# Attention and MoE on one core: first-block outputs with queries on partitions, held and rationed MoE work

## The chip, the cores and the metric

The kernel runs on one core of a Trainium2 chip. The metric is the device time of that core in microseconds (us), the median of several executions. Engines are TensorE (PE; PEld is its weight load), VectorE (DVE), ScalarE (ACT), GpSimd (POOL) and SyncE (SP, which only issues DMAs here). A DMA is a transfer between DRAM and the memory on the core; it is issued by an engine and lands some us later. Results of matmuls stand in PSUM, a part of that memory. On one core an execution is called slow when it lies over 1.5% above the fastest of its kernel; such runs are left out of every ratio.

## The reference, cut to what matters

```python
# q, k, v: [8 batches, 8 heads, 576, 64]; f: [8, 8, 576]; w_in: [512, 2048]; w_out: [2048, 512]
scores = q @ k.T / sqrt(64) + (cum[i] - cum[j])      # cum = cumsum(log(clip(f)))
scores = where(j > i, -1e9, scores)
attn   = exp(scores - max) / (sum + 1e-9)
x      = (attn @ v) as [8 * 576, 512]
out    = silu(x @ w_in) @ w_out                      # float32, [4608, 512]
```

The decay is folded into per-key weights `w`: v is multiplied by `w`, and the softmax denominator is the sum of `w * exp(score)`.

## The kernel before: the parts that matter

The 576 queries of a batch are split: the first 128 (the "first block") of all eight batches are done early, two or four batches at a time, so that the MoE (here the two matmuls with w_in and w_out and the silu between them) has input early; the other 448 are done in a main loop of 16 quads (a quad is four heads of one batch, two quads to a batch). In between the scores of a quad, the function `fill(us)` emits MoE work: first-matmul chunks ("hp": four matmuls, then tanh on ACT, then the product "gt" on VectorE) and second-matmul parts ("po": four matmuls of 512 columns). Each engine's instructions stand in its queue in the order in which this program emits them. Scores and attention outputs share two PSUM tiles; hp, po and a few others share four PSUM buffers.

```python
    def out0(b):                     # first block: features on partitions
        dn = psc.tile([P, 2, 512], FP32, name="dn0", tag="sc")
        ...                          # 24 matmuls: 8 denominators broadcast to 32 rows, 16 halves of v
        nc.vector.reciprocal(out=rec, in_=dn[:, 0 : 2 * P])          # 128 x 256
        nc.vector.tensor_tensor(out=xg(g)..., in0=dn[:, 2 * P : 6 * P]..., in1=rec..., op=ALU.mult)

    def step():                      # one chunk of MoE work
        a, c = at["m1"], at["m2"]
        can1 = a < len(M1) and M1[a][0] in ready        # first matmul: group's x was emitted
        ...
        if can1 and can2:
            f1 = M1[a][1] / NFC                         # share done of the first-matmul group
            f2 = (c - sum(M2_OF[:g2])) / M2_OF[g2]      # share done of the second-matmul group
            can1 = f1 <= f2 or g1 > g2 + 1
        ...

    FILL = 2.6
    for m in range(NQ):              # main loop, one quad each
        n = 2 * m
        scores(n, 0); scores(n, 1); prepare(n);     fill(FILL)       # (joined lines)
        scores(n, 2); scores(n + 1, 0); prepare(n + 1); fill(FILL)
        scores(n + 1, 1); scores(n + 1, 2);         fill(FILL + 1.0)
        finish_quad(m)               # attention matmuls, denominator to SBUF, two reciprocals of 128 x 224
        fill(FILL)
        for e in range(2):
            divide(m, e, nc.gpsimd)  # x = numerator * reciprocal, on POOL
        if m % 2 == 1:
            ready.add(REST_OF[m // 2])                  # from here on, hp of this batch may be emitted
            ...
```

The loads, in the order in which POOL issues them: q and k of the first four blocks, the first half of w_in, (v of the first blocks is scaled), q and k of blocks 4 and 5, the other half of w_in, all of w_out. After w_out has landed, SP starts loading for the main loop.

The softmax here doesn't subtract the row's maximum and nothing guards it: scores larger than these inputs give would overflow.

## Time and profile before

| | before |
|---|---|
| time, median | 405.99 us (4 runs) |
| span of the profiled run (an execution of 404.22 us, not one of the four) | 402.4 us |
| TensorE busy | 349.2 us, 87% |
| first MoE matmul | 27.63 us |
| first scores of the main loop | 80.3 us |
| from there to the end | 322.1 us |

The page's first part gives busy time, share of the span and number of instructions of each engine. Its second part cuts the span into 40 slices; a digit is a share in tenths, and PEclk is the TensorE clock that was granted.

```profile
PE 349.2 (87%) x3682; PEld 192.7 (48%) x3717; DVE 208.6 (52%) x310; ACT 235.7 (59%) x408; POOL 151.7 (38%) x252
...
PEclk9958999999969999996999899999899989999999
```

TensorE has the most work, but an eighth of its span is idle, and the clock is below full in many slices all along the kernel. The list of waits of TensorE says what ended its idle time (engine, line, what it waited for: us in total, times, longest).

```profile
PE hp L478 <- POOL x L460: 20.5, 14, 2.7
...
PE hp L478 <- DVE x L321: 4.9, 2, 4.0
```

The first line is the largest: 20.5 us before first-matmul chunks, waiting for x, the product on POOL; the second, 4.9 us, is the same for the first blocks, where VectorE makes x. The timeline around one such wait (start us, duration us, engine, line, operation, count, and in brackets the idle time before with what ended it):

```profile
107.03 0.61 PE L429 MATMUL dn<-u,vp 128*32 128x128 bf16 x24
...
107.65 2.97 DVE L452 RECIPROCAL rec<-rec 128x224 f32<-128x224 f32 x2 [4.16 <-ACT rec L444]
108.10 0.40 PE L398 MATMUL sc<-qkT 64*128 64x128 bf16 x8 [0.46 <-ACT nm L447]
...
108.84 0.50 PE L478 MATMUL hp<-x,w_in_bf 128*128 128x384 bf16 x2
...
110.79 2.73 POOL L460 TENSOR_TENSOR x<-nm,rec 128x384 bf16<-128x384 f32 x4 [3.66 <-DVE rec L452]
112.06 0.48 PE L478 MATMUL hp<-x,w_in_bf 128*128 128x384 bf16 x1 [2.72 <-POOL x L460]
...
113.29 4.32 PE L478 MATMUL hp<-x,w_in_bf 128*128 128x384 bf16 x13 [0.75 <-POOL x L460]
```

The attention matmuls end at 107.6. Nothing but two sets of scores stands before the first chunk that needs the result. The two reciprocals take 2.97 us, POOL begins at 110.79, and TensorE stands still for 2.72 and 0.75 us. Then the thirteen matmuls from 113.29 take 4.32 us, 0.33 us each; in an undisturbed stretch sixteen of the same shape take 2.77 us, 0.17 each. A table of stretches (length; busy us of PE, PEld, DVE, ACT, POOL; clock; DMA share; GB/s) shows why:

```profile
105.00:110.00 5.00, 3.85 (x99) 2.35 (x98) 2.35 (x2) 3.94 (x7) 2.05 (x3) 1.00 1.09 226
...
113.00:118.00 5.00, 4.71 (x19) 2.07 (x20) 1.66 (x3) 1.83 (x4) 2.80 (x8) 0.50 0.32 66
```

After the gap the clock is 0.50. The same happens in the next batches. The start has another loss; of the timeline from 25 us:

```profile
25.10 1.75 DVE L317 RECIPROCAL rec<-dn 128x256 f32<-128x256 f32 x1
...
27.63 0.59 PE L478 MATMUL hp<-x,w_in_bf 128*128 128x512 bf16 x1 [3.95 <-DVE x L321]
...
28.43 10.71 PE L478 MATMUL hp<-x,w_in_bf 128*128 128x512 bf16 x38 [0.22 <-DMA w_in_bf<-in_moe_w_in_dram]
```

VectorE is the busy engine here, with a reciprocal of 1.75 us for each block, and the first hp waits for its product. Two marks for later, of the queue of SP and of TensorE: the small marker load that is issued once w_out has landed, and the first scores of the main loop.

```profile
48.89 0.50 SPq L188 DMA_DIRECT2D junk<-w_out_bf  x1
...
80.30 0.40 PE L398 MATMUL sc<-qkT 64*128 64x128 bf16 x8
```

### The profile page before, as it was taken

What the parts mean: (1) busy time and instruction counts of PE and PEld (TensorE: products, weight loads), DVE (VectorE), ACT (ScalarE), POOL (GpSimd) and SP (SyncE); (2) the same over time, 40 slices, a digit from 0 to 9 for tenths busy, and PEclk for the clock granted to TensorE, in tenths of its full rate; (3) what the DMA queues carried; (4) which work ended last, traced back from release to release, by engine and by line L of the source; (5) the groups of instructions that cost most, each with busy time, mean ns of one, the idle gap of its engine ahead of it and who ended that gap; (6) DMA issues with size and microseconds to landing.
All of it is one profiled execution on the core that took longest, in us unless ns stands there. A gap on an engine that the chain in (4) does not pass through costs nothing.

```text
span 402.4 us, 9181 instructions
## 1 busy us (share of the span) xinstructions
PE 349.2 (87%) x3682; PEld 192.7 (48%) x3717; DVE 208.6 (52%) x310; ACT 235.7 (59%) x408; POOL 151.7 (38%) x252
## 2 busy tenths in 40 slices
PE   3639799899879959996995999999799989979995
PEld 3524475455435435543543555555355445545652
DVE  2776881745437335623653483665536546355330
ACT  3515562385747648664864776868568667544441
POOL 8384035203640941454084227519506531120000
PEclk9958999999969999996999899999899989999999
DMA  9989979484849348573925664388394430000112
GB/s 165 165 134 177 199 170 199 120 173 113 174 96 158 89 115 167 76 190 76 183 64 143 134 110 112 88 176 174 84 190 92 119 71 30 29 26 28 52 46 61
DMA packets 140955, 47.96 MB, mean 119 GB/s; under 512 B 131120, under 2 KB 135216, under 8 KB 140912
## 3 DMA queue, kind: packets, MB, share of 16 engines
q1 hardware_dynamic: 132272, 41.06, 47.6%
q0 software_dynamic: 8640, 6.31, 10.4%
q8 instruction: 29, 0.48, 0.5%
q14 instruction: 14, 0.11, 0.1%
HBM read 36.85 MB, written 9.44 MB: 115 GB/s over the span
## 4 chain that ended last, share of the span: by engine, by line
PE 67%; DVE 9%; issue 6%; ACT 6%; DMA 5%; POOL 4%; SPq 2%; POOLq 0%; ACTq 0%
PE po L504 28%; PE hp L478 27%; PE dn L429 6%; PE sc L398 5%; DMA vf<-in_v_dram 4%; DVE rec L452 4%; POOL x L460 3%; ACT u L405 2%; DVE gt L487 2%; DVE rec L317 2%; ACT th L486 1%; ACT rec L444 1%; DMA w_in_bf<-in_moe_w_in_dram 1%; SPq L127 1%; DVE x L321 1%
## 5 line engine op out<-in xcount | busy, mean ns | idle before, releaser
L478 PE MATMUL hp<-x,w_in_bf 128*128 128x384 bf16 (+2 forms) x829 | 156.2, 332 | 30.3 <-POOL x L460 20.5
L487 DVE SCALAR_TENSOR_TENSOR gt<-th,hp 128x384 bf16<-128x384 bf16 (+2 forms) x208 | 103.0, 518 | 87.2 <-ACT th L486 84.9
L486 ACT ACTIVATE th<-hp 128x384 bf16<-128x384 f32 (+2 forms) x208 | 94.6, 473 | 80.7 <-PE hp L478 74.9
L504 PE MATMUL po<-w_out_bf,gt 128*128 128x512 bf16 x544 | 135.1, 381 | 3.0 <-issue 1.0
L478 PEld LDWEIGHTS <-w_in_bf 128*128 128x128 bf16 x832 | 81.9, 102 | 96.3 <-issue 52.9
L460 POOL TENSOR_TENSOR x<-nm,rec 128x384 bf16<-128x384 f32 x64 | 46.3, 754 | 171.8 <-DVE rec L452 171.8
L405 ACT ACTIVATE u<-sc 128x1024 bf16<-128x1024 f32 (+1 forms) x96 | 89.6, 988 | 19.0 <-PE sc L398 18.7
L504 PEld LDWEIGHTS <-gt 128*128 128x128 bf16 x576 | 54.3, 98 | 57.3 <-issue 4.8
L452 DVE RECIPROCAL rec<-rec 128x224 f32<-128x224 f32 x32 | 47.4, 1524 | 38.5 <-ACT rec L444 38.5
L410 DVE TENSOR_TENSOR u<-u,maskf 128x1024 bf16<-128x1024 bf16 x32 | 27.1, 846 | 36.5 <-ACT u L405 36.4
L513 ACT ACTIVATE osb<-po 128x512 f32<-128x512 f32 x36 | 21.7, 603 | 29.3 <-PE po L504 29.1
L354 POOL TENSOR_TENSOR vp<-vf,w_bf 128x512 bf16<-128x512 f32 (+1 forms) x32 | 33.9, 1067 | 5.5 <-DMA vf<-in_v_dram 4.9
L398 PE MATMUL sc<-qkT 64*128 64x128 bf16 (+3 forms) x384 | 23.2, 242 | 2.0 <-ACT nm L447 2.0
L398 PEld LDWEIGHTS <-qkT 64*128 64x128 bf16 x384 | 14.1, 97 | 15.9 <-issue 12.6
L444 ACT ACTIVATE rec<-dn 128x448 f32<-128x448 f32 x16 | 8.7, 544 | 19.8 <-PE dn L429 19.8
L429 PE MATMUL dn<-u,vp 128*32 128x128 bf16 (+3 forms) x768 | 19.7, 237 | 0.0
L335 POOL CAST qkb<-qf 128x384 bf16<-128x384 f32 x32 | 18.4, 574 | 0.8 <-PE hp L478 0.5
L429 PEld LDWEIGHTS <-vp 128*32 128x32 bf16 x768 | 16.5, 97 | 3.6
L251 PE MATMUL tp<-sel,qkb 128*64 128x64 bf16 x256 | 10.9, 278 | 6.7 <-DMA qkb<-in_q_dram 5.7
L335 POOL CAST qkb<-kf 128x384 bf16<-128x384 f32 x32 | 16.6, 519 | 0.3 <-DMA kf<-in_k_dram 0.2
L290 POOL TENSOR_TENSOR v<-vf,w_bf 128x512 bf16<-128x512 f32 x8 | 8.7, 1097 | 18.9 <-DMA vf<-in_v_dram 15.5
L447 ACT ACTIVATE nm<-dn 128x448 f32<-128x448 f32 x32 | 15.6, 544 | 0.0
(50 smaller groups left out, 163.9 us busy)
## 6 DMA issues: line engine op xcount, KB each, us to landing
vf<-in_v_dram SPq DMA_DIRECT2D x32, 256.0 KB, 4.6
out_dram<-osb SPq DMA_DIRECT2D x32, 256.0 KB, 2.3
qf<-in_q_dram SPq DMA_DIRECT2D x64, 96.0 KB, 3.1
kf<-in_k_dram SPq DMA_DIRECT2D x64, 96.0 KB, 2.8
w_in_bf<-in_moe_w_in_dram POOLq DMA_DIRECT2D x8, 256.0 KB, 11.6
w_out_bf<-in_moe_w_out_dram POOLq DMA_DIRECT2D x4, 512.0 KB, 15.1
qkb<-in_q_dram POOLq DMA_DIRECT2D x8, 128.0 KB, 5.8
qkb<-in_k_dram POOLq DMA_DIRECT2D x8, 128.0 KB, 6.5
```

What stands on the lines that cost most here:

```text
L335: nc.gpsimd.tensor_copy(out=t2[:, c0 : c0 + NR, :].rearrange("p c x -> p (c x)"), in_=t[:, :, :, :].rearrange("p c h d -> p (c h d)"),)
L354: nc.gpsimd.tensor_tensor(out=vp[r, c, :, :], in0=vst[b][c][r, :, :], in1=w_bf[r, c + 1, b * H : (b + 1) * H, None].to_broadcast([n, H, D] ...
L398: nc.tensor.matmul(sc[:, i, o - c0 : o - c0 + q1 - q0], lhsT=kt, rhs=t[r, q0:q1], start=True, stop=True,)
L405: nc.scalar.activation(out=u[:, :, c0:c1], in_=sc[:, :, 0 : c1 - c0], func=ACT.Exp, scale=scale)
L410: nc.vector.tensor_tensor(out=x, in0=x, in1=maskf[:, None, :].to_broadcast([P, 2, SM]), op=ALU.mult)
L429: nc.tensor.matmul(dn[HD * j : HD * (j + 1), q0:q1], lhsT=w, rhs=us[n][:, i, o : o + q1 - q0], start=(kb == 0), stop=(kb == NM),)
L452: nc.vector.reciprocal(out=recs[qd][:, r], in_=recs[qd][:, r])
L460: eng.tensor_tensor(out=xg(g)[:, cc, g0 : g0 + c1 - c0], in0=nm[:, c0:c1], in1=rec[:, c0:c1], op=ALU.mult,)
L478: nc.tensor.matmul(hp[:, :], lhsT=w_in_bf[:, cc, fc * P : (fc + 1) * P], rhs=xg(g)[:, cc, :], start=(cc == 0), stop=(cc == NCC - 1),)
L486: nc.scalar.activation(out=th[:, :], in_=hp[:, :], func=ACT.Tanh, scale=0.5)
L487: nc.vector.scalar_tensor_tensor(out=gt[:, fc, :], in0=th[:, :], scalar=1.0, in1=hp[:, :], op0=ALU.add, op1=ALU.mult,)
L504: nc.tensor.matmul(po[:, :], lhsT=gt[:, fc, tb * P : (tb + 1) * P], rhs=w_out_bf[:, fc, :], start=(fc == 0), stop=(fc == NFC - 1),)
```

## The change

Its intent: (1) take the wide reciprocal off VectorE by computing the first blocks with queries on partitions, where a denominator is one column, and transpose the result back on TensorE; (2) start the scan that gives `w` first, and issue the weight loads later and in other portions; (3) in the main loop, hold a batch's chunks back by two slots, so that other work stands where TensorE used to wait, and give smaller portions of MoE work, so that there is some left; (4) put one divide of a batch's last quad on VectorE. Core of the diff:

```diff
     def out0(b):
-        ...                                            # 24 matmuls
-        nc.vector.reciprocal(out=rec..., in_=dn[:, 0 : 2 * P])
-        nc.vector.tensor_tensor(out=xg(g)..., ...)
+        dn = psc.tile([P, 2, 4, P], FP32, name="dn0", tag="sc")
+        for h in range(H):                             # v0 has a 65th column, the weight
+            nc.tensor.matmul(dn[:, h // 4, h % 4, 0 : D + 1],
+                             lhsT=u[:, h % 2, h // 2, :], rhs=v0[b][:, h, :], ...)
+        nc.vector.reciprocal(out=rec[:, :, :], in_=dn[:, :, :, D])       # 128 x 8
+        for g in range(2):
+            nc.vector.tensor_tensor(out=xq..., in0=dn..., in1=rec..., op=ALU.mult)
+    def back0(b):
+        for cc in range(NCC):
+            nc.tensor.transpose(tx[:, cc, :], xq[:, cc, :], ident_bf[:, :])
+        nc.scalar.copy(out=xg(g)[:, :, c0 : c0 + P], in_=tx[:, :, :])
 ...
+    weights_scan()
     turn0(0)
-    weights_scan()
     turn0(1)
-    scores0(0)
     weights()
-    load_w_in(0)
+    scores0(0)
     convert_v0(0)
     turn0(2)
+    convert_v0(1)
+    load_w_in(0, W1)
+    out0(0)
     scores0(1)
-    convert_v0(1)
-    out0(0)
 ...                                    # w_out: now after convert_v0(4) and (5)
+    def slot(us_):
+        fill(us_)
+        for x in pending:
+            x[0] -= 1
+        while pending and pending[0][0] == 0:
+            ready.update(pending.pop(0)[1])
     for m in range(NQ):
+        piece = 1.5 if m < 2 else 2.5
 ...                                    # every fill(FILL ...) becomes slot(piece)
-        for e in range(2):
-            divide(m, e, nc.gpsimd)
-            ready.add(REST_OF[b])
+        divide(m, 0, nc.gpsimd)
+        divide(m, 1, nc.vector if last else nc.gpsimd)
+            pending.append([2, gs])                    # ready two slots later
```

More of the change, by code (lines that the diff above doesn't have):

```diff
@@ L62 @@
     recp = ctx.enter_context(tc.tile_pool(name="recp", bufs=2))
+    xqp = ctx.enter_context(tc.tile_pool(name="xqp", bufs=2))
     nmp = ctx.enter_context(tc.tile_pool(name="nmp", bufs=4))
@@ L80 @@
     kT0 = [const.tile([P, NP, P], BF16, name=f"kT0_{b}") for b in range(B)]
-    v0 = [const.tile([P, H, D], BF16, name=f"v0_{b}") for b in range(B)]
+    v0 = [const.tile([P, H, D + 1], BF16, name=f"v0_{b}") for b in range(B)]
     GW = [4 * P, 2 * P, 2 * P] + [RB] * NM + [NM * ST] + [RB] * (B - NM) + [(B - NM) * ST]
@@ L169, with load_w_in @@
     w_in_v = moe_w_in.rearrange("(g j e r) f -> g e j r f", g=NCC // 2, j=4, e=2)
-    def load_w_in(i):
-        c0, c1 = i * DFF // 2, (i + 1) * DFF // 2
+    def load_w_in(c0, c1):
         for cc in range(NCC):
@@ L289, in convert_v0 @@
     def convert_v0(b):
+        w = w_bf[:, 0, b * H : (b + 1) * H, None]
         nc.gpsimd.tensor_tensor(
-            out=v0[b][:, :, :],
+            out=v0[b][:, :, 0:D],
             in0=vf0.pop(b)[:, :, :],
-            in1=w_bf[:, 0, b * H : (b + 1) * H, None].to_broadcast([P, H, D]),
+            in1=w.to_broadcast([P, H, D]),
             op=ALU.mult,
         )
+        nc.gpsimd.tensor_copy(out=v0[b][:, :, D : D + 1], in_=w)
+    xqs: dict[int, bass.AP] = {}
     def out0(b):
-        dn = psc.tile([P, 2, 512], FP32, name="dn0", tag="sc")
@@ L299, in out0 @@
-        dn = dn[:, :, :].rearrange("p a x -> p (a x)")
-        for what in range(3):
-            for g in range(2):
-                for j in range(4):
-                    h = 4 * g + j
-                    if what == 0:
-                        w = w_bf[:, 0, b * H + h : b * H + h + 1].to_broadcast([P, HD])
-                    else:
-                        w = v0[b][:, h, (what - 1) * HD : what * HD]
-                    c0 = (2 * what + g) * P
-                    nc.tensor.matmul(
-                        dn[HD * j : HD * (j + 1), c0 : c0 + P],
-                        lhsT=w,
-                        rhs=u0[b][:, h % 2, h // 2, :],
-                        start=True,
-                        stop=True,
-                    )
@@ L316, in out0 @@
-        rec = recp.tile([P, 2, P], FP32, name="rec", tag="rec")
-        nc.vector.reciprocal(
-            out=rec[:, :, :].rearrange("p g t -> p (g t)"), in_=dn[:, 0 : 2 * P]
-        )
-        g, c0 = HEADS_OF[b]
-        nc.vector.tensor_tensor(
-            out=xg(g)[:, :, c0 : c0 + P].rearrange("p (g e) t -> p e g t", e=2),
-            in0=dn[:, 2 * P : 6 * P].rearrange("p (e g t) -> p e g t", e=2, g=2),
-            in1=rec[:, None, :, :].to_broadcast([P, 2, 2, P]),
-            op=ALU.mult,
-        )
+        dn = psc.tile([P, 2, 4, P], FP32, name="dn0", tag="sc")
@@ new lines, in out0 @@
+        u = u0.pop(b)
+        for h in range(H):
+            nc.tensor.matmul(
+                dn[:, h // 4, h % 4, 0 : D + 1],
+                lhsT=u[:, h % 2, h // 2, :],
+                rhs=v0[b][:, h, :],
+                start=True,
+                stop=True,
+            )
+        rec = recp.tile([P, 2, 4], FP32, name="rec0", tag="rec0")
+        nc.vector.reciprocal(out=rec[:, :, :], in_=dn[:, :, :, D])
+        xq = xqp.tile([P, 2, 2, 4, HD], BF16, name="xq", tag="xq")
+        for g in range(2):
+            nc.vector.tensor_tensor(
+                out=xq[:, g, :, :, :].rearrange("p e j r -> p j e r"),
+                in0=dn[:, g, :, 0:D].rearrange("p j (e r) -> p j e r", e=2),
+                in1=rec[:, g, :, None, None].to_broadcast([P, 4, 2, HD]),
+                op=ALU.mult,
+            )
@@ L330, in cast_qk @@
+        xqs[b] = xq
+    def back0(b):
+        xq = xqs.pop(b)[:, :, :, :, :].rearrange("p g e j r -> p (g e) (j r)")
+        tx = pbig.tile([P, NCC, P], BF16, name="tx", tag="big")
+        for cc in range(NCC):
+            nc.tensor.transpose(tx[:, cc, :], xq[:, cc, :], ident_bf[:, :])
+        g, c0 = HEADS_OF[b]
+        nc.scalar.copy(out=xg(g)[:, :, c0 : c0 + P], in_=tx[:, :, :])
     def cast_qk(n):
@@ L563, in fill @@
         return True
+    W1 = DFF // 2
+    weights_scan()
     turn0(0)
-    weights_scan()
     turn0(1)
-    scores0(0)
     weights()
@@ L573 @@
     gpool = ctx.enter_context(tc.tile_pool(name="gpool", bufs=2))
-    load_w_in(0)
+    scores0(0)
     convert_v0(0)
     turn0(2)
+    convert_v0(1)
+    load_w_in(0, W1)
+    out0(0)
     scores0(1)
-    convert_v0(1)
-    out0(0)
     turn0(3)
+    convert_v0(2)
+    back0(0)
+    out0(1)
     scores0(2)
-    convert_v0(2)
-    out0(1)
+    convert_v0(3)
+    back0(1)
+    out0(2)
     scores0(3)
-    convert_v0(3)
-    out0(2)
+    back0(2)
     out0(3)
+    back0(3)
     ready.add(0)
+    load_w_in(W1, W1 + W1 // 2)
+    load_qk0(4)
+    load_qk0(5)
+    load_w_in(W1 + W1 // 2, DFF)
     nc.gpsimd.memset(maskf[:, P + 2 * P : SM], 1.0)
@@ L593 @@
         nc.gpsimd.tensor_copy(out=maskf[:, c * P : (c + 1) * P], in_=maskf[:, 0:P])
-    load_qk0(4)
-    load_qk0(5)
-    load_w_in(1)
-    for i in range(WQ):
-        load_w_out(i)
-    after(w_in_bf[0:1, NCC - 1, DFF // 2 - 16 : DFF // 2])
+    after(w_in_bf[0:1, NCC - 1, W1 - 16 : W1])
     load_v0(4)
@@ L604, with two_more @@
     load_v0(7)
+    def two_more(b, piece):
+        turn0(b)
+        turn0(b + 1)
+        scores0(b)
+        fill(piece)
+        scores0(b + 1)
+        fill(2 * piece)
+        out0(b)
+        fill(piece)
+        out0(b + 1)
+        fill(piece)
+        back0(b)
+        fill(piece)
+        back0(b + 1)
+    fill(7.0)
+    convert_v0(4)
+    convert_v0(5)
+    for i in range(WQ):
+        load_w_out(i)
     after(w_out_bf[0:1, NFC - 1, DM - 16 : DM])
@@ L611 @@
         load_v(0, c)
-    fill(8.0)
-    for b in (4, 5):
-        turn0(b)
-    scores0(4)
-    convert_v0(4)
-    scores0(5)
-    convert_v0(5)
-    fill(1.5)
-    out0(4)
-    out0(5)
+    two_more(4, 0.9)
     load_qk0(6)
     load_qk0(7)
+    while at["m1"] < NFC:
+        step()
     ready.add(1)
@@ L628 @@
     open2["w"] = True
-    fill(9.0)
-    for b in (6, 7):
-        turn0(b)
-    scores0(6)
+    fill(8.0)
     convert_v0(6)
-    scores0(7)
     convert_v0(7)
-    fill(1.5)
-    out0(6)
-    out0(7)
-    ready.add(2)
+    two_more(6, 0.9)
     cast_qk(0)
@@ L646 @@
     load_tails(1)
-    fill(6.0)
+    while at["m2"] < M2_OF[0]:
+        step()
+    ready.add(2)
+    fill(2.0)
     def prepare(n):
@@ L666, in prepare @@
                 convert_v(b + 1, c)
-    def finish_quad(m):
+    pending: list = []
+    def slot(us_):
[4 more added lines that the diff above has]
+            ready.update(pending.pop(0)[1])
+    for m in range(NQ):
+        n = 2 * m
+        piece = 1.5 if m < 2 else 2.5
+        scores(n, 0)
+        scores(n, 1)
+        prepare(n)
+        slot(piece)
+        scores(n, 2)
+        scores(n + 1, 0)
+        prepare(n + 1)
+        slot(piece)
+        scores(n + 1, 1)
+        scores(n + 1, 2)
+        slot(piece)
         attend(m)
@@ L671, in finish_quad @@
         rec_part(m, 1)
-    FILL = 2.6
-    for m in range(NQ):
-        n = 2 * m
-        scores(n, 0)
-        scores(n, 1)
-        prepare(n)
-        fill(FILL)
-        scores(n, 2)
-        scores(n + 1, 0)
-        prepare(n + 1)
-        fill(FILL)
-        scores(n + 1, 1)
-        scores(n + 1, 2)
-        fill(FILL + 1.0)
-        finish_quad(m)
-        fill(FILL)
-        for e in range(2):
-            divide(m, e, nc.gpsimd)
-        if m % 2 == 1:
+        slot(piece)
+        last = m % 2 == 1
+        divide(m, 0, nc.gpsimd)
+        divide(m, 1, nc.vector if last else nc.gpsimd)
+        if last:
             b = m // 2
-            ready.add(REST_OF[b])
-            if b in (NM - 1, B - 1):
-                ready.add(TAILS_OF[b][0])
+            gs = [REST_OF[b]] + ([TAILS_OF[b][0]] if b in (NM - 1, B - 1) else [])
+            pending.append([2, gs])
+    for x in pending:
+        ready.update(x[1])
     while step() is not None:
```

## The prediction

> **What bounds the kernel now.** TensorE is the resource (page: 349.2 of 402.4 us busy, 87%), yet the loss lies where it stands still and then runs at half clock.
>
> 1. Start. The timeline has the first MoE matmul at 27.6 us. VectorE is full from 15 to 27 us: each first block costs it a reciprocal of 128x256 (1.75 us), a product (0.69), a mask (0.69) and a cast (0.68). The first MoE matmuls then run at clock 0.50 until about 33 us (windows). At 48.4 to 50.9 TensorE stands 2.5 us because VectorE does two more such reciprocals.
>
> 2. Main loop. The waits list 20.5 us, 14 times, of "hp" for the POOL divide of x: after the second quad of a batch the program goes straight from the attention matmuls to the first MoE chunk that needs this quad. The chain shows the path: denominator copy, two reciprocals (2.97 us), POOL products (1.07 us for 128x384). Four gaps are about 3.5 us (at 109, 145, 181, 217), three about 2 us (287, 321, 356). After six of them 13 or so matmuls run at about 0.32 instead of 0.17 us (windows: clock 0.50 to 0.58), some 1.8 us lost each. The Trainium skill, "TensorE: Matmul & The Clock Gate", Part 1, says that the clock halves after an idle window of about 3.4 us and returns after as much work; this trace shows about 4.5 us at half clock after each long gap.
>
> **What the change does.** First blocks: 24 matmuls per block (0.7 us) become 8 narrow ones plus 4 transposes (estimate 0.5); the reciprocal has 8 columns (estimate 0.15), the product is two of 256 (estimate 0.8 together); ScalarE gets a copy of 128x512 (0.59, as the qkT cast). VectorE per block drops from 3.8 to 2.3 us, but only what precedes the first MoE work and the 48-us stall is critical. The scan goes first: weights about 2 us earlier. w_in is requested later (13 instead of 7 us), but the queue is then empty; it should land about 21, no later than x. I estimate the first MoE matmul at 23.5 us, still cold: gain 4; the removed stalls bring it to 7.5 when the main loop starts.
>
> Main loop: the new batch's chunks come free two slots later, after some 5 us of other work; one divide goes to VectorE, so x is ready about 4 us after the attention matmuls. All seven gaps should vanish: 20 us plus 10 of half clock. Charges: in the first two quads only 6 us of MoE work stand against 11 us of ScalarE work (TensorE idles about 2 us each), and in slots of four 128x384 chunks ScalarE (2 exps of 1.0, 4 tanh of 0.5) exceeds TensorE's 3.3 us. Together about 7 us given back. ScalarE rises to 26 of 29 to 30 us per batch, the near second limit.
>
> Sum: 405.5 - 7.5 - 30 + 7 = 375 us, range 364 to 388. Faster by over 2%: 0.95; within: 0.04; slower: 0.01.
>
> **Expected profile.** Span about 372; TensorE above 90% busy, its busy time falling to about 336 us; waits of hp on x under 4 us; period of a middle batch from 36 to about 30 us; clock about 0.98; first hp near 23.5 us; the pure MoE tail longer (65 instead of 50 us), dense.
>
> **What would make this wrong.** w_in landing late (first hp waits on DMA near 27 us); ScalarE or VectorE order (gt behind two reciprocals) holding the four shared PSUM buffers, so that gaps return as waits on th or gt; too little second-matmul work in the held slots, leaving gaps that still drop the clock; loads not keeping up with 30 us per batch.

## The result and the profile after

| | before | after |
|---|---|---|
| time, median (4 runs each) | 405.99 us | 374.85 us |
| span of the profiled run | 402.4 | 373.9 |
| first MoE matmul | 27.63 | 26.31 |
| first scores of the main loop | 80.3 | 79.7 |
| from there to the end | 322.1 | 294.2 |

The ratio is 0.924 (95% interval 0.9191 to 0.9289). Ratios here are the mean time of one kernel's fast runs over that of the other's fast runs of the same rounds, so they are not quite the ratio of the medians quoted beside them.

The last two rows already say where the gain is: the first main-loop scores come 0.6 us earlier, and the same amount of MoE work has been emitted before them in both programs; the rest of the kernel is 27.9 us shorter (322.1 - 294.2). The page after:

```profile
PE 343.8 (92%) x3621; PEld 190.4 (51%) x3621; DVE 206.5 (55%) x334; ACT 237.4 (64%) x416; POOL 148.0 (40%) x248
...
PEclk9957999969999999999999999999999999999998
```

The clock is now below full in the first quarter alone, but for the last slice. In the table of stretches TensorE is busy 100% from 232 to 306 us. The waits after:

```profile
PE hp L482 <- DVE gt L491: 8.3, 10, 1.4
...
PE hp L482 <- ACT osb L517: 2.8, 1, 2.8
```

No wait on the POOL product is left. A new one stands in its place: 8.3 us in ten pieces, waiting for gt. Its pattern, of TensorE's timeline around the attention matmuls of a batch's first quad (113.36 to 115.4):

```profile
113.36 0.81 PE L433 MATMUL dn<-u,w_bf 128*32 128x448 bf16 x28
...
114.82 0.61 PE L433 MATMUL dn<-u,vp 128*32 128x128 bf16 x24
115.37 2.12 PE L482 MATMUL hp<-x,w_in_bf 128*128 128x384 bf16 x12
118.92 0.81 PE L482 MATMUL hp<-x,w_in_bf 128*128 128x384 bf16 x4 [1.43 <-DVE gt L491]
```

Three chunks (12 matmuls) run, the fourth waits 1.43 us. No matmul here runs at half clock. The period of a batch in the middle, read from the chain of waits as the start of the reciprocals of one kind, is 146.65 to 177.24, 30.6 us, where it was 35.5 (145.31 to 180.84).

The start after, in order of time, POOL, VectorE and TensorE mixed:

```profile
15.01 2.71 POOL L174 DMA_DIRECT2D w_in_bf<-in_moe_w_in_dram  x4
...
18.87 1.04 POOL L291 TENSOR_TENSOR v<-vf,w_bf 128x512 bf16<-128x512 f32 x1
...
18.95 1.51 DVE L285 TENSOR_TENSOR u<-u,maskf 128x1024 bf16<-128x1024 bf16 x1 [0.39 <-ACT u L278]
...
25.67 0.59 ACT L330 COPY x<-tx 128x512 bf16<-128x512 bf16 x1 [2.42 <-PE tx L328]
...
26.31 1.01 PE L482 MATMUL hp<-x,w_in_bf 128*128 128x512 bf16 x2 [0.67 <-ACT x L330]
...
28.51 9.70 PE L482 MATMUL hp<-x,w_in_bf 128*128 128x512 bf16 x33 [0.23 <-DMA w_in_bf<-in_moe_w_in_dram]
...
40.47 3.10 POOL L182 DMA_DIRECT2D w_out_bf<-in_moe_w_out_dram  x4
```

x is complete at 26.26 (25.67 + 0.59), but the chunks of w_in, issued from 15.01 to 17.72, have not all landed: the weight load of the matmul at 28.51 is the last to wait on DMA. Dense hp work begins at 28.51; before, it began at 28.43. w_out is issued from 40.47 on. SP waits for it and only then loads for the main loop:

```profile
58.37 0.50 SPq L188 DMA_DIRECT2D junk<-w_out_bf  x1
...
73.54 1.58 SPq L520 DMA_DIRECT2D out_dram<-osb  x3
75.23 2.98 SPq L372 DMA_TRANSPOSE qkT<-qkb  x2
```

In the kernel before, the same small marker load, which tells that w_out has landed, stood at 48.89, now at 58.37. The transposes of q and k for the first scores are issued at 75.23, and the stores of finished outputs, in the same queue, at 73.54. TensorE there:

```profile
78.30 1.01 PE L482 MATMUL hp<-x,w_in_bf 128*128 128x256 bf16 x4 [2.81 <-ACT osb L517]
79.68 0.61 PE L402 MATMUL sc<-qkT 64*128 64x128 bf16 x8 [0.37 <-DMA qkT<-qkb]
...
80.60 1.89 PE L508 MATMUL po<-w_out_bf,gt 128*128 128x512 bf16 x4
```

It waits 2.81 us (ScalarE cannot copy a finished output out of PSUM before an output buffer is stored; SP issued these stores only at 73.54, behind its loads for the main loop) and 0.37 us (transposes), and the four matmuls at 80.60 take 1.89 us where the four at 74.03 took 1.03: half clock again.

### The profile page after: what moved, and what is told of

Its sections match the earlier page's. It is cut to its first block, busy times and chain, and to the rows that moved or that the text cites. A ratio compares the mean times of both kernels' runs of the same rounds, so it can differ in the third digit from the quotient of the medians.

```text
span 373.9 us, 9022 instructions
## 1 busy us (share of the span) xinstructions
PE 343.8 (92%) x3621; PEld 190.4 (51%) x3621; DVE 206.5 (55%) x334; ACT 237.4 (64%) x416; POOL 148.0 (40%) x248
## 3 DMA queue, kind: packets, MB, share of 16 engines
q0 software_dynamic: 10752, 6.31, 11.6%
## 4 chain that ended last, share of the span: by engine, by line
PE 67%; DMA 14%; DVE 6%; ACT 4%; SPq 3%; issue 3%; POOL 2%; ACTq 0%; POOLq 0%
PE po L508 29%; PE hp L482 23%; PE dn L433 8%; PE sc L402 6%; DMA w_out_bf<-in_moe_w_out_dram 4%; DMA vf<-in_v_dram 4%; DVE rec L456 4%; DMA w_in_bf<-in_moe_w_in_dram 3%; SPq L143 2%; ACT u L409 2%; DMA qkb<-in_q_dram 2%; DVE gt L491 1%; ACT th L490 1%; DMA qkT<-qkb 1%; POOL v L291 1%
## 5 line engine op out<-in xcount | busy, mean ns | idle before, releaser
L482 PE MATMUL hp<-x,w_in_bf 128*128 128x384 bf16 (+2 forms) x832 | 150.8, 320 | 12.5 <-DVE gt L491 8.3
L508 PE MATMUL po<-w_out_bf,gt 128*128 128x512 bf16 x576 | 143.2, 381 | 0.0
L482 PEld LDWEIGHTS <-w_in_bf 128*128 128x128 bf16 x832 | 78.9, 99 | 73.6 <-issue 21.9
L464 POOL TENSOR_TENSOR x<-nm,rec 128x384 bf16<-128x384 f32 (+1 forms) x48 | 35.2, 761 | 123.5 <-DVE rec L456 114.1
L339 POOL CAST qkb<-qf 128x384 bf16<-128x384 f32 x32 | 17.5, 546 | 9.5 <-DMA qf<-in_q_dram 9.4
L339 POOL CAST qkb<-kf 128x384 bf16<-128x384 f32 x32 | 19.8, 619 | 1.3 <-DMA kf<-in_k_dram 1.3
## 6 DMA issues: line engine op xcount, KB each, us to landing
w_in_bf<-in_moe_w_in_dram POOLq DMA_DIRECT2D x4, 256.0 KB, 10.7
```

Source lines behind the costliest of these rows:

```text
L339: nc.gpsimd.tensor_copy(out=t2[:, c0 : c0 + NR, :].rearrange("p c x -> p (c x)"), in_=t[:, :, :, :].rearrange("p c h d -> p (c h d)"),)
L464: eng.tensor_tensor(out=xg(g)[:, cc, g0 : g0 + c1 - c0], in0=nm[:, c0:c1], in1=rec[:, c0:c1], op=ALU.mult,)
L482: nc.tensor.matmul(hp[:, :], lhsT=w_in_bf[:, cc, fc * P : (fc + 1) * P], rhs=xg(g)[:, cc, :], start=(cc == 0), stop=(cc == NCC - 1),)
L508: nc.tensor.matmul(po[:, :], lhsT=gt[:, fc, tb * P : (tb + 1) * P], rhs=w_out_bf[:, fc, :], start=(fc == 0), stop=(fc == NFC - 1),)
```

## The experiments

Twelve kernels ran, all with correct results. The useful number besides the time is the length from the first main-loop scores to the end of the profiled run, because the start varies by a few us from run to run with the landing of loads (80.5 in one run and 85.1 in another with the same first part). It is read from one trace of each kernel; the two traces of the changed kernel differ by 0.7 us. Here it is for all with a usable profile. The ratio is to the runs of before on the same chip (medians 403.83 to 404.42), the time is a median:

| kernel | time us | ratio to before | first main-loop score | from there to the end |
|---|---|---|---|---|
| before | 405.99 | 1 | 80.3 | 322.1 |
| after | 374.85 | 0.924 | 79.7 | 294.2 |
| new main loop only | 374.19 | 0.9239 | 80.5 | 290.1 |
| new first part only | 403.37 | 0.998 | 80.7 | 322.4 |
| hold only | 379.51 | 0.9387 | 80.7 | 296.7 |
| rationing only | 381.39 | 0.9412 | 80.1 | 297.5 |
| hold and rationing | 374.66 | 0.9249 | 85.1 | 290.1 |
| gaps filled with idle matmuls | 394.6 | 0.9757 | 82.6 | 311.4 |
| after, again | 374.78 | 0.9262 | 79.4 | 293.5 |
| after, w_in early (e6) | 372.46 | 0.9197 | 77.5 | 294.1 |
| after, w_in and w_out early (e7) | 368.12 | 0.9099 | 72.8 | 292.1 |
| after, reciprocals split | 374.95 | 0.9264 | 79.5 | 293.4 |
| early loads (e7), evenly mixed | 363.43 | 0.9001 | 74.5 | 287.3 |
| the same, blocks reordered | 365.23 (one run of 1195.88 in it) | 0.9014 | see below | see below |

### Which half carries the gain

The first two kernels cross the halves: the old first part with the new main loop, and the reverse.

```diff
 # e1: kernel before
-    FILL = 2.6 ... old main loop
+    pending, slot(), piece ... new main loop, with the divide on VectorE
 # e2: kernel after
-    new main loop
+    old main loop
```

> The kernel before with only the new main loop (held groups, finer rationing, one divide on VectorE); first blocks and loads as before. Theory (from the two traces: the first score matmul of the main loop stands at 80.3 us before and 79.7 us after, so nearly all of the gain lies in the main loop): about 376 us, within 1.5% of the changed kernel. Rival (the recorded prediction: 7.5 us of the gain come from the first blocks): about 382 us or more.

> The changed kernel with the old main loop. Theory: within 1% of before, 402 to 407 us, with the seven waits of hp on the POOL divide back (about 20 us). Rival (recorded prediction): about 398 us.

Measured: 374.19 us (ratio 0.9239, 0.9195 to 0.9283; one of its four runs, 380.07, was slow and is left out of the ratio) and 403.37 us (ratio 0.998, 0.9938 to 1.0022). The new main loop alone has the whole gain; the new first part alone has none that can be measured. (The same new main loop takes 290.1 us behind the old first part and 294.2 behind the new one, where TensorE runs at half clock from 79.7 to 84 and waits on gt, in the traces from 86 us on, for 8.3 instead of 6.4 us; why the waits are longer there was not traced.) In the second kernel the old wait is back at its old size:

```profile
PE hp L482 <- POOL x L464: 20.5, 14, 2.7
```

### What in the main loop carries it: hold, rationing or divide

Three parts were tried on the kernel before. The hold alone delays `ready` by two slots and leaves all else. Rationing alone takes the smaller pieces and leaves `ready` at once. The third kernel has both, with all divides still on POOL.

```diff
 # e3: hold only
-            ready.add(REST_OF[b])
+            pending.append([2, gs])
 # e10: rationing only
-        fill(FILL) ... fill(FILL + 1.0) ... fill(FILL)
+        fill(piece) in each of the four places, piece = 1.5 if m < 2 else 2.5
 # e9: both
```

> The kernel before with only the two-slot hold; fills stay 2.6, 2.6, 3.6, 2.6 us and both divides stay on POOL. Theory (the hold needs second-matmul work left over for the held slots, which only the finer rationing leaves): waits of hp on x vanish, but TensorE then waits for ScalarE between the scores in the first four batches, gaps of 2 to 4 us and half clock stay; about 393 to 398 us. Rival (the hold alone is the gain): about 377 us.

> The kernel before with the finer rationing but no hold, both divides on POOL. In the built program one or two second-matmul parts (0.9 us each) now stand after the attention matmuls, before the chunk that needs x, where before there were none. Theory: the seven waits on x shrink by about 1 to 1.7 us each but stay, 8 to 14 us in all; the clock still drops in some; about 388 to 394 us. Rival (the rationing alone is worth nothing): 402 to 406 us.

> The kernel before with the hold and the finer rationing, both divides on POOL, old first blocks. It stands between the hold alone (379.5 us) and the whole new main loop (374.2). Theory (once chunks are held, no one waits for x, so which engine divides does not matter): 374 to 375 us, ratio to before 0.924 to 0.928. Rival (the VectorE divide gives the last 5 us): about 379 us, ratio 0.938.

Measured: hold 379.51 us, rationing 381.39, both 374.66. Two of the three expectations missed, in the same direction: each part alone has most of the gain. From the main-loop lengths, the hold alone saves 25.4 us, rationing alone 24.6, both 32.0. They overlap, since either can fill the same gap. With both, the divide on VectorE adds nothing (290.1 with and without it): once nobody waits for x, it does not matter which engine makes it.

My reason for expecting little of the hold alone was that nothing would be left to emit. The trace shows what I had overlooked:

```profile
108.51 0.40 PE L398 MATMUL sc<-qkT 64*128 64x128 bf16 x8 [0.46 <-ACT nm L447]
...
110.83 0.40 PE L398 MATMUL sc<-qkT 64*128 64x128 bf16 x8 [0.41 <-ACT u L405]
111.75 0.37 PE L398 MATMUL sc<-qkT,kT 64*128 64x448 bf16 x2 [0.52 <-ACT u L405]
112.67 0.61 PE L398 MATMUL sc<-qkT 64*128 64x320 bf16 x4 [0.55 <-ACT u L405]
113.21 5.43 PE L478 MATMUL hp<-x,w_in_bf 128*128 128x384 bf16 x24
```

In the kernel before, the held-up chunk stood in front of the remaining scores of the next quad, which were ready to run; they stood behind it in TensorE's queue and ran only after it, at 117.54, and ScalarE waited with them. With the hold, these scores go through, at the pace of ScalarE (waits of 0.41 to 0.71 us here, 7.0 us in the whole run), and when the chunks come, x is there (waits on it in the whole run: 1.7 us). The clock stays higher than before: the table of stretches gives 0.95 from 110 to 145 and 1.00 in the stretches after it up to 340, where the kernel before has 0.90 to 0.95 up to 240 and 0.94 to 0.99 from there to 340.

Rationing alone leaves one or two second-matmul parts (0.9 us each) to be emitted between the attention matmuls and the first chunk, which shortens the four long waits; the three later ones are gone.

```profile
PE hp L478 <- POOL x L460: 9.2, 8, 1.8
```

That is the wait on x in the list of waits (total us, count, longest). On the timeline of TensorE in the same run, the matmuls after two of the gaps:

```profile
139.51 1.62 PE L478 MATMUL hp<-x,w_in_bf 128*128 128x384 bf16 x9 [1.35 <-POOL x L460]
...
200.19 3.04 PE L478 MATMUL hp<-x,w_in_bf 128*128 128x384 bf16 x9 [1.35 <-POOL x L460]
```

The waits fall from 20.5 to 9.2 us, within the 8 to 14 expected. The clock was the part that I mis-sized: after two of the four gaps (139.51, 169.78) nine matmuls take 1.62 us, full speed; after the one at 200.19 they take 3.04, and after the first gap the clock is 0.50 too (104.18 to 111.01). The saving is not fully accounted for: 11.3 us of waits and at most 10.7 us of half clock (next section) are less than the 24.6 us.

### What the half clock costs

To separate the wait from the slower matmuls after it, idle matmuls on old data fill the gap in the kernel before. The first real matmul starts its accumulation anew, so the result is unchanged.

```diff
         hp = pbig.tile([P, w], FP32, name="hp", tag="big")
+        if fc == 0 and g in WARM:              # 20 (b = 0..3) or 10 (b = 5, 6, 7)
+            for _ in range(WARM[g]):
+                nc.tensor.matmul(hp[:, :], lhsT=w_in_bf[:, 0, 0:P], rhs=w_in_bf[:, 0, 0:w],
+                                 start=True, stop=True)
```

> The kernel before, with 20 (three later groups: 10) matmuls of 128x384 on old data put before the first MoE chunk of a batch, so that TensorE is busy in the gap; the real chunk overwrites their result. Theory (half clock after a gap costs about 1.8 us in each of six): the waits on x stay near zero in the trace because dummies fill them, the clock stays at 1.00, about 395 us, 2.5% faster. Rival (the half clock costs nothing, or something else sets the pace): 404 to 407 us.

Measured: 394.6 us, ratio 0.9757 (0.9716 to 0.9797). The same gap:

```profile
111.18 3.42 PE L480 MATMUL hp<-w_in_bf 128*128 128x384 bf16 x20
114.44 0.65 PE L488 MATMUL hp<-x,w_in_bf 128*128 128x384 bf16 x3
115.63 2.27 PE L488 MATMUL hp<-x,w_in_bf 128*128 128x384 bf16 x13 [0.54 <-POOL x L460]
```

The chunk of thirteen matmuls takes 2.27 us instead of 4.32, and x comes no earlier; 4.1 us of waits on x remain in the run. The main-loop length falls from 322.1 to 311.4: 10.7 us of the kernel before were half clock alone, against the 10 of the prediction. So a kernel that adds useless work is 2.4% faster here. The Trainium skill, "TensorE: Matmul & The Clock Gate", Part 1, gives 3.4 us as the idle window after which the clock halves; the gaps before were 2.72 plus 0.75 us with one matmul between, and some of about 2 us in pieces had the same effect, so a pause well short of an empty 3.4 us could do it in this case. The 10.7 us are 2.7% of the span of 402.4.

The traces show more closely which gaps do it. In all of them that have a clock record the granted clock changes only at whole multiples of 3.41 us from its first change (in the main loop of the kernel before it stays at half for 3.41 or 6.83 us). So count back 3.41 us from each drop, and take the same grid around the gaps that caused none. In the kernel before and the rationing-only kernel, TensorE was busy for 0.32 to 1.68 us (9 to 49%) of the 3.41 us before each of the eight drops in the main loop, and for 2.02 to 2.22 us (59 to 65%) of the three such windows with a wait on x that left the clock full. The limit thus seems to lie near half, and not at an empty window; no run was made to test it, and in the kernel with only the new main loop one window of 49% (364.22 to 367.63) left the clock full.

### Why the first part gave nothing

The traces suggest the loads. In the changed kernel POOL issues w_in 8 us later than before (15.0 against 7.1) and w_out 13 us later (40.5 against 27.2), because both now stand behind the scaling of v blocks. For w_in this waits for the decay weights (POOL idles 5.21 us until 12.3), for w_out it waits for the loads of v (2.26 and 2.13 us). Two kernels move them back:

```diff
 # e6
+    load_w_in(0, W1)
     scores0(0)
     convert_v0(0)
     turn0(2)
     convert_v0(1)
-    load_w_in(0, W1)
 # e7: e6, and
     load_w_in(W1 + W1 // 2, DFF)
+    for i in range(WQ):
+        load_w_out(i)
 ...
     convert_v0(4)
     convert_v0(5)
-    for i in range(WQ):
-        load_w_out(i)
```

> The changed kernel again, unedited, so that the three edits of this set are compared with it on one chip. Both theories: ratio to before 0.92 to 0.93, about 374 us.

> The changed kernel with the first half of w_in requested before the first v blocks are converted, as the kernel before does. Theory (the first blocks gained nothing because weight loads come later: w_in issued at 15 to 18 us landed at 28.4, and w_out issued at 40.5 to 43 landed at 58.4, which held the first scores of the main loop to 79.7): first hp no longer waits on DMA and starts at about 26.3 us when x is ready, w_out lands 6 to 9 us earlier, first main-loop score at 75 to 76, time 370 to 371 us. Rival (the order chain exp, mask, matmul of the new blocks sets the start, loads do not matter): within 1 us of the changed kernel.

> As the w_in edit, and w_out is requested right after the last part of w_in, before the v blocks 4 and 5 are converted. Theory: w_out lands at about 46 to 50 us, first main-loop score at 75 us, time 369 to 371 us; if the w_in edit alone already frees w_out, no more than 1 us better than it. Rival: no change against the changed kernel.

Measured, on one chip: the changed kernel again 374.78 us (0.9262), w_in early 372.46 (0.9197), both early 368.12 (0.9099). With w_in early, the first hp starts at 24.44 and no hp waits on DMA, 2 us better than I expected, but w_out still lands at 55.4 (3 us earlier, not 6 to 9) and the first main-loop scores come at 77.5, so only a part of it reaches the end. With both:

```profile
50.68 0.50 SPq L188 DMA_DIRECT2D junk<-w_out_bf  x1
```

That is the timeline of the SP queue in the run with both loads early; its timeline of TensorE shows the start of the main loop:

```profile
71.37 0.60 PE L482 MATMUL hp<-x,w_in_bf 128*128 128x256 bf16 x4 [0.26 <-ACT osb L517]
72.75 0.40 PE L402 MATMUL sc<-qkT 64*128 64x128 bf16 x8 [0.79 <-DMA qkT<-qkb]
```

w_out has landed by 50.68, the wait for the output buffer has shrunk from 2.81 to 0.26 us, the main loop starts at 72.75, and the kernel gains 6.7 us (374.78 - 368.12). This is the gain that the rewritten first blocks were meant to give; in the changed kernel it was spent on waiting for weights. That e6 alone was not enough was a partial miss of my expectation (370 to 371); e7 came out a little better than expected (369 to 371). Which part of the rewrite (queries on partitions, the scan first, the new order of the later blocks) makes the start faster once the loads are early was not separated.

What the prediction had wrong was when w_in is requested and how fast it lands when nothing else is under way. The page's list of DMA issues (what, queue, count, size, median us to landing), before and after:

```profile
w_in_bf<-in_moe_w_in_dram POOLq DMA_DIRECT2D x8, 256.0 KB, 11.6
```

```profile
w_in_bf<-in_moe_w_in_dram POOLq DMA_DIRECT2D x4, 256.0 KB, 10.7
```

The list counts the bytes written, as bf16. Before, other loads were under way; after, the DMA engines were nearly empty when the four loads were requested (share 0.10 from 13 to 15 us, 0.18 from 15 to 17), and yet the median is 10.7 us instead of 11.6. From 19 to 29 us the share is 0.83 or more in each step of 2 us, with these loads, from 20.46 with the next part of w_in and from 24.43 with q and k of later blocks. From the first request at 15.01 to SP's marker at 28.48, which says that all four have landed, it took 13.5 us; the prediction had a request at 13 and a landing 8 us later. The Trainium skill, "DMA: Bandwidth & Descriptors", "Anatomy of one DMA", gives a fixed 2 us plus bytes at 436 GB/s for a DMA issued from POOL, which for one load of 256 KB is an estimated 2.6 us, and for the four taken as one load of 1 MB an estimated 4.4 us. The 13.5 us are three times that.

### The new wait on gt

Two ideas were tried. The first: gt stands behind two reciprocals on VectorE, so place these apart.

```diff
         attend(m)
-        rec_part(m, 0)
-        rec_part(m, 1)
-        slot(piece)
+        if m % 2 == 1:
+            rec_part(m, 0); rec_part(m, 1); slot(piece)
+        else:
+            fill(piece / 2); rec_part(m, 0); slot(piece / 2); rec_part(m, 1)
```

> The changed kernel, but in the first quad of each batch the two reciprocal halves are placed in the middle and at the end of the slot after the attention matmuls, not both before it. Theory (TensorE's 8.3 us of waits of hp on the gt product come from gt standing behind 3 us of reciprocals on VectorE, all four PSUM buffers being held): these waits fall to 2 to 4 us, time 370 us, 1% faster than the changed kernel. Rival (ScalarE with 26 us per batch is the true limit and the wait only moves to it): within 0.5% of the changed kernel.

Measured: 374.95 us, ratio 0.9264, the same as the changed kernel beside it (0.9262). The waits on gt fell only to 7.3 us, and 0.9 us came up before po. My expectation fell. The second idea: after the hold, `step` finds the second matmul ahead and emits first-matmul chunks alone until they have caught up, four to a slot. Four chunks take all four PSUM buffers, and the next cannot start before the oldest has passed ScalarE, where it stands behind two exps of about 1 us, and VectorE. So mix both kinds evenly, on top of the early loads:

```diff
+            if M1[a][1] == 0:
+                base[g1] = (g2, f2)                    # second-matmul share when this group starts
+            g0, f0 = base.get(g1, (g2, 0.0))
+            if g0 == g2 and f0 < 1.0:
+                f2 = (f2 - f0) / (1.0 - f0)
             can1 = f1 <= f2 or g1 > g2 + 1
```

> The early-loads version (w_in and w_out early, 368.1 us), with first and second matmul chunks mixed evenly after the hold instead of first-matmul chunks alone until they have caught up. Theory (8.3 us of waits of hp on gt come from slots of four first chunks, which take all four PSUM buffers while ScalarE does two exps and VectorE the reciprocals; splitting the reciprocals alone did not help): these waits fall to 3 to 5 us, time 364 to 366 us, ratio to before 0.90. Rival (the wait moves again): 367 to 369 us.

Measured: 363.43 us, ratio 0.9001 (0.8947 to 0.9054), and

```profile
PE hp L482 <- DVE gt L491: 3.6, 4, 1.4
```

The waits on gt fall from 8.3 to 3.6 us, and the main-loop length from 292.1 to 287.3. This is the fastest version, 3.0% below the changed kernel on the same chip (363.43 against 374.78). That the burst of four chunks causes the wait is shown by this pair; that ScalarE's exps and not VectorE make up most of it was argued from the order of instructions and from the failed split, and is not shown by itself.

### Reordering the first blocks

```diff
-    out0(0)
     scores0(1)
+    out0(0)
     turn0(3)
     convert_v0(2)
-    back0(0)
-    out0(1)
     scores0(2)
+    back0(0)
+    out0(1)
 ...                                    # the same for blocks 2 and 3
```

> As the evenly mixed version, and in the first four blocks the scores of block b+1 stand before the output matmuls of block b, so that exp and mask of the next block overlap the division of this one. Theory (in the changed kernel these blocks run at 3.0 to 3.4 us each because score, exp, mask and output matmul follow one another in TensorE order): first hp at about 21 to 23 us instead of 24.4, time 1 to 2 us below the evenly mixed version. Rival (the qkT transposes, which follow the w_out load, set the start of the main loop): first hp earlier, first main-loop score unchanged, same time within 0.3%.

Measured: fast runs 362.93 to 366.53 us, ratio 0.9014 (0.8969 to 0.9059), against 0.9001 without the reordering: no gain, as the rival said. The profiled execution was of another kind: it took 1195.88 us.

```profile
PE 1181.6 (99%) x3621; PEld 435.6 (36%) x3621; DVE 207.9 (17%) x334; ACT 254.2 (21%) x416; POOL 136.3 (11%) x248
```

```profile
L508 PE MATMUL po<-w_out_bf,gt 128*128 128x512 bf16 x576 | 498.6, 1101 | 0.0
```

The first line is the page's busy time of each engine in this run. The second line is the group of second-matmul instructions: count, busy us and mean ns of one. A po matmul took 498.6 / 576 = 0.866 us of TensorE on average, four times the 0.216 us of a po matmul in an undisturbed stretch (four in 0.86 us in the chain after). TensorE was 99% busy. The records hold no change of the clock: the page has no clock row and the listing of cores gives 1.000. It happened once in 6 runs of this kernel and in none of the others. Whether the first hp came earlier is therefore not shown; the times alone say that it did not help.

## Why the prediction was right, and where it was not

The total was right: 375 predicted, 374.85 measured, inside 364 to 388. Step by step:

- **Waits on x vanish, 20 us.** Right. 20.5 us of waits before, none in the list after, and back to 20.5 with the old main loop.
- **Half clock, 10 us.** Right in kind and size: 10.7 us by the kernel with idle matmuls. The "about 4.5 us at half clock after each long gap" was no fixed length: from the end of the four long gaps it lasted 5.2, 3.2, 5.2 and 3.1 us.
- **Who does it.** The prediction took hold, rationing and the VectorE divide together. Hold or rationing alone gives about 25 of 32 us, and the divide nothing.
- **"About 7 us given back".** Two charges were named. The first, about 2 us of idle time in each of the first two quads, did not come: from 79.7 to 110 TensorE idles 0.5 us in all. The second, slots of four chunks, is where the loss is, as 8.3 us of waits on gt, which the prediction listed under what could go wrong. In net terms the charge was too large: the new main loop on the old first part is 32.0 us shorter, more than 30 - 7 = 23.
- **"First MoE matmul at 23.5 us", "it should land about 21".** This step failed. x was complete only at 26.26, 2.8 us late, and w_in landed only by 28.5: it was requested at 15.0 and not at 13, and took 13.5 us from there, not 8, although the DMA engines were nearly empty at the request.
- **"The removed stalls bring it to 7.5 when the main loop starts".** Failed as a consequence: 0.6 us. The 2.5 us stall at 48 us did go, but w_out landed 9.5 us later than before (58.37 against 48.89) and held the main loop's loads. With the loads early, the main loop starts at 72.75, 7.6 us before the old 80.3 (at 74.5 in the trace of the evenly mixed version, which has the same first part); so the compute side of that term was sized about rightly, and the order of loads took it away.
- **The sum.** About 7 us too much at the start (0.6 instead of 7.5) and about 5 too little in the main loop (27.9 instead of 23) nearly cancelled. What is left is the starting point: the prediction subtracted from a median of 405.5, but the trace that it was read from belongs to an execution of 404.22. The right total is partly luck.
- **Other marks.** Period of a batch 30.6 (predicted 30); TensorE 92% busy (above 90); its busy time 343.8, not 336, of which the half clock from 79.7 to 84 is some 2 us and the rest was not traced; clock 0.969 in the profiled run, but 0.978 to 0.982 in the other three (0.98); the MoE tail from the last attention matmuls at 306.3 to the end is 67.6 us (65).

VectorE's relief in the first blocks was real (a reciprocal of 0.21 instead of 1.75 us, products of 0.76 instead of 0.69), but TensorE's part did not shrink: 0.43 plus 0.40 us for matmuls and transposes against 0.29 plus 0.41. And the blocks then ran at 3.0 to 3.4 us each, because scores, exp, mask and output matmuls of successive blocks follow one another in TensorE's order. One of the masks took 1.51 us where about 0.7 is usual (the kernel before has one of 1.49 us too): it began at 18.95, POOL's product on v ran from 18.87 to 19.91, and after 0.55 us more the mask was done. The Trainium skill, "SBUF — State Buffer", "SBUF: two separate sides", says that a VectorE operation with two inputs in SBUF (the memory on the core) and a GpSimd operation that reads SBUF lock each other out of a shared port pair; these times agree with it, though no run here tests it.

## What to carry to other kernels

A matmul that had to wait here also held the ready scores emitted behind it (from 108.9 to 117.5 in the kernel before); ask what ready work stands behind each long wait, and put it in front, and ration independent work so that some is left for that place. A gap on TensorE costs its length and then the half clock after it, which here was another half of the gap. Before counting on a faster compute stage, look at the issue times of the loads that the next stage needs: here a stage was freed of 7 us and gave back all of it until two loads were issued earlier.

## What the Trainium skill lacked or had wrong

- "TensorE: Matmul & The Clock Gate", Part 1: names an idle window of about 3.4 us. In the rationing-only run a gap of 0.60 and 1.43 us of waiting left the clock full (nine matmuls in 1.62 us) and one of 0.81 and 1.35 us in the same execution did not (3.04 us); the section gives no share of busy time that would tell the two apart. In the two traces that were counted, windows of 3.41 us with 9 to 49% busy time were followed by half clock and those with 59 to 65% were not.
- The same page, "Seeing it yourself", tells of a clock stuck at a quarter "for 50+µs". Here a whole execution of 1195 us had matmuls four times as long (0.866 us), and no clock record showed it. The page warns that such records are unreliable, but not that this may last for a whole execution with no record at all.
- "DMA: Bandwidth & Descriptors", "Anatomy of one DMA": its formula is for one load and gives an estimated 4.4 us for 1 MB. Here four loads of 256 KB, requested together from POOL with the DMA engines nearly empty, took 13.5 us until all had landed (median of one 10.7 us). These loads read float32 and write bf16, and the page gives no time for such loads.
